# A memory-bound decode kernel: two loads for w4's apart rows, two for wo, and another order of the first loads on two issuing engines

## The chip, the cores and the metric

The kernel runs on one core of one Trainium2 chip. Times are device microseconds (us) of one execution. A timed execution is about 1.8 us longer than the span of the profile, which goes from the first to the last instruction.

## The reference

One decode step for four sequences, in bfloat16, with two branches on one normalised input:

```python
x  = A_x                                   # 4 x 1 x 576
xn = layernorm(x)
out = x + A(xn) + B(xn)

# A: attention over the last 2048 of 8192 cached positions; 32 query heads, 16 kv heads, 128 wide
q = xn @ wq                                # wq 576 x 4096
p = softmax(q @ k_window / sqrt(128))      # k, v: 4 x 16 x 2048 x 128
A = (p @ v_window) @ wo                    # wo 4096 x 576

# B: with one position, the shifted mixer part is zero, so x1 = xn
B = xn + gelu(layernorm(xn) @ w3) @ w4     # w3 576 x 4608, w4 4608 x 576
```

The K and V windows are 67 MB of the 87.17 MB that a run reads. Each weight is used for four rows only.

## The kernel before

Everything is streamed once from memory. The sync engine issues nearly all loads; six buffers of 2 MB hold K and V heads. The parts that the change and the argument touch:

```python
kvp = ctx.enter_context(tc.tile_pool(name="kv", bufs=NKV))        # NKV = 6
wop = ctx.enter_context(tc.tile_pool(name="wo", bufs=2))
# ... cut: the other pools
first = wop.tile([P, WOR * D], BF16, tag="wo", name="first")      # small things of the start share a wo buffer

# the first loads
x_bf = part(D, B)                                                 # a slice of "first"
nc.scalar.dma_start(out=x_bf[:], in_=x2)                          # 4.5 KB
nc.sync.dma_start(out=wq_sb[:, KJ * NQ:], in_=...)                # wq's last 64 rows, 128 pieces of 4096 bytes
nc.sync.dma_start(out=wq_sb[:, 0:KJ * NQ], in_=wq_main)           # 128 rows of 32,768 bytes

def load_wo(p):                                                   # a quarter of wo, one buffer
    t = wop.tile([P, WOR, D], BF16, tag="wo", name="wo_sb")
    nc.sync.dma_start(out=t[:].rearrange("p i n -> p (i n)"), in_=wo_src[p])

# 128 rows of w4 ("apart rows") are loaded by eight small DMAs: "A" 20 x 5 rows, "C" 12 rows, six of 2 or 4 rows
X_AFTER = {13: ["A", (0, 0, 4)], 14: [(1, 0, 4), (2, 0, 2), "C"], 15: [(2, 2, 4), (3, 0, 2), (3, 2, 4)]}

# the order of loads: K0 K1 K2 V0 K3 V1 K4 V2 ..., a wo quarter before V0, V4, V8, V12, w3 after V2, w4 last
def flush_loads():
    while pos["n"] < len(order) and pos["free"] > 0:
        kind, h = order[pos["n"]]
        if kind == "V" and h % WOQ == 0:
            load_wo(h // WOQ)
        # ... cut: load_kv(kind, h), and the apart rows after V13, V14 and V15
    if pos["n"] == len(order):
        pos["n"] += 1
        load_w4()                                                 # six pieces, the last two are small

# ... cut: 16 heads of scores, softmax and PV; the MLP's first product at head 7
# the end
mlp_extra(XC, XS)          # apart rows A and C, before the last head's PV
# ... cut: the last PV and its sums
mlp_extra(XB, XC)          # the single apart rows
o_proj(hl)
for lo, hi in pieces:
    mlp_out(lo, hi)        # w4, piece by piece as it lands
# ... cut: two halves of acc to fin
nc.sync.dma_start(out=o2, in_=fin[:])
```

Of the kernel before, what the change touches and what calls it, by code (L numbers as in the profile page):

```python
# [22 lines left out]
def kernel(  # L23
# [15 lines left out]
    P = 128  # L39
# [38 lines left out]
    wp = ctx.enter_context(tc.tile_pool(name="w", bufs=1))  # L78
    wop = ctx.enter_context(tc.tile_pool(name="wo", bufs=2))
    ktp = ctx.enter_context(tc.tile_pool(name="kt", bufs=2))  # L80
# [16 lines left out]
    WOQ = WOH // rep  # L97
    wo_src = A_wo.rearrange("(s p i) n -> s p (i n)", p=P, i=WOR)

# [6 lines left out]

    first = wop.tile([P, WOR * D], BF16, tag="wo", name="first")
    cut = {"at": 0}

    def part(n, parts=P):  # L110
# [3 lines left out]
        return first[0:parts, lo:lo + n]  # L114

    x_bf = part(D, B)
    nc.scalar.dma_start(out=x_bf[:], in_=x2)
    wq_sb = wp.tile([P, KJ * NQ + NQ // 2], BF16, tag="w", name="wq_sb")
    wq_main = A_wq[0:KJ * P, :].rearrange("(p j) n -> p (j n)", j=KJ)
    nc.sync.dma_start(out=wq_sb[:, KJ * NQ:], in_=A_wq[KJ * P:D, :].rearrange("r (e f) -> (r e) f", e=2))  # L120
    nc.sync.dma_start(out=wq_sb[:, 0:KJ * NQ], in_=wq_main)

    def load_wo(p):
        t = wop.tile([P, WOR, D], BF16, tag="wo", name="wo_sb")
        nc.sync.dma_start(out=t[:].rearrange("p i n -> p (i n)"), in_=wo_src[p])
        wo_tiles[p] = t
# [9 lines left out]
    X0 = F - P  # L136
    XB, XC, XA = 0, 4, 5
    XS = 10
    NX = 20
    NS = NFM + XS  # L140

    def x_cols(ap):
        b, c, a = ap[:, 0:16], ap[:, 16:28], ap[:, 28:P]
        return [(0, b.rearrange("p (q i) -> p i q", q=4)), (16, c.rearrange("p (q g) -> p g q", q=4)),
                (28, a.rearrange("p (q g i) -> p i g q", q=4, g=5))]

# [12 lines left out]

    def x4_rows(part):  # L160
        t = w_tiles["x4"]
        if part == "A":
            src = B_w4[X0 + 28:F, :].rearrange("(q g i) n -> g q (i n)", q=4, g=5)
            nc.sync.dma_start(out=t[0:NX, XA * D:XS * D], in_=src)
        elif part == "C":
            src = B_w4[X0 + 16:X0 + 28, :].rearrange("(q g) n -> g q n", q=4)
            nc.sync.dma_start(out=t[0:12, XC * D:XA * D], in_=src)
        else:
            q, lo, hi = part
            src = B_w4[X0 + 4 * q + lo:X0 + 4 * q + hi, :].rearrange("(q i) n -> q (i n)", q=1)  # L170
            nc.sync.dma_start(out=t[q:q + 1, (XB + lo) * D:(XB + hi) * D], in_=src)

    X_AFTER = {13: ["A", (0, 0, 4)], 14: [(1, 0, 4), (2, 0, 2), "C"], 15: [(2, 2, 4), (3, 0, 2), (3, 2, 4)]}

# [295 lines left out]
    def o_proj(h):  # L470
        if h % WOQ < WOQ - 1:
            return
        acc_matmuls([(op[:, i, :], wo_tiles[h // WOQ][:, i, :]) for i in range(WOR)])

# [35 lines left out]
    def mlp_turn(r):  # L510
# [9 lines left out]
        if r < 2:  # L520
            dst = xs[:, r * NFH:r * NFH + 16, :].rearrange("p (g u) b -> p u g b", u=n)
        else:
            e1 = slice(QD, 2 * QD)
            for s in range(XS):
                off, k = (4 * s, 4) if s < XC else (16, 12) if s == XC else (28 + NX * (s - XA), NX)
                nc.tensor.transpose(out=gT_all[0:k, n * m + s, :], in_=g_x[e1, off:off + k],
                                    identity=ident_f[e1, e1])
            for lo, hi, k in ((XB, XC, 4), (XC, XA, 12), (XA, XS, NX)):
                nc.scalar.activation(out=xs[0:k, NFM + lo:NFM + hi, :],
                                     in_=gT_all[0:k, n * m + lo:n * m + hi, 0:B], func=ACT.Copy)  # L530
            nc.scalar.activation(out=xs[:, NFM - 1, :], in_=gT_ps[:, 0, 1, 0:B], func=ACT.Copy)
            nc.scalar.activation(out=xs[:, 16:18, :], in_=gT_ps[:, :, 0, 0:B], func=ACT.Copy)  # L532
            return
# [10 lines left out]

    def mlp_extra(lo, hi):
        t = w_tiles["x4"]
        acc_matmuls([(gT[0:k, NFM + s, :], t[0:k, s * D:(s + 1) * D])
                     for s in range(lo, hi) for k in (4 if s < XC else 12 if s == XC else NX,)])

# [6 lines left out]
    for h in range(Hkv):  # L556
        order.append(("V", h))
        if h + 3 < Hkv:
            order.append(("K", h + 3))
        if h == min(X_AFTER):  # L560
            order.append(("X", h))
    W3_AFTER = ("V", 2)
    pos = {"n": 0, "free": NKV}

    def flush_loads():
        while pos["n"] < len(order) and pos["free"] > 0:
            kind, h = order[pos["n"]]
            if kind == "V" and h % WOQ == 0:
                load_wo(h // WOQ)
            if kind == "X":  # L570
                load_x4()
            else:
                load_kv(kind, h)
            if kind == "X" or kind == "V" and h > min(X_AFTER):
                for part in X_AFTER.get(h, []):
                    x4_rows(part)
            pos["n"] += 1
# [82 lines left out]
    o_scale(hl - 1)  # L660
    mlp_extra(XC, XS)
    for s in range(NSL):
# [8 lines left out]
    o_pick(hl)  # L671
    mlp_extra(XB, XC)
    o_proj(hl)
# [41 lines left out]
```

## Time and profile before

| | before |
|---|---|
| median, lowest to highest of the first 3 runs | 211.31 us, 211.28 to 212.18 |
| span of the profiled run, mean granted TensorE clock | 209.6 us, 0.868 |
| bytes read, rate over the span | 87.17 MB, 416 GB/s |
| busy share: PE, DVE, ACT | 72%, 54%, 17% |
| w4's first piece issued, last load complete | 189.67 us, 206.60 us |

Two more rows are needed: the page's part on DMA queues (packets, MB, and the time of their packets as a share of 16 engines' span) tells which ring carried what.

```profile
q1 hardware_dynamic: 6684, 87.17, 97.7%
q10 hardware_dynamic: 8, 0.00, 0.0%
```

q1 is the ring of the sync engine, q10 that of ScalarE. Before the change q10 carries x and nothing else. The table of busy time by stretches reads: stretch, us, then busy us and instructions of PE, PEld, DVE, ACT, POOL, then the granted clock, the DMA share and GB/s.

```profile
0.00:2.00 2.00, 0.00 (x0) 0.00 (x0) 0.60 (x2) 0.68 (x1) 1.26 (x9) 1.00 0.17 22
2.00:4.00 2.00, 0.00 (x0) 0.00 (x0) 1.01 (x4) 1.99 (x4) 0.17 (x3) 1.00 1.29 504
4.00:14.00 10.00, 3.45 (x23) 1.32 (x27) 4.19 (x16) 5.03 (x4) 5.26 (x16) 1.00 0.95 405
```

In the third stretch every engine is already at work: x is there at 2.9 us, long before wq.

### The profile page before, as it was taken

The numbers are of one execution on the slowest core, as the hardware profiler recorded it, in microseconds if no ns is written. First come the engines' busy times: TensorE is split into PE (matmuls) and PEld (weight loads), VectorE is DVE, ScalarE is ACT, GpSimd is POOL, SyncE is SP. The second block draws the span as 40 slices with busy tenths as digits, with TensorE's granted clock in tenths as the row PEclk, the third lists the DMA queues.
The fourth block names the chain that finished last, engine by engine and source line by source line (L and its number), as shares of the span: only waits on it lengthen the run. The fifth ranks groups of instructions, "written<-read, shape, count | busy, mean of one in ns | idle before, by whom it ended". The sixth has DMA issues, their size and how long they took to land.

```text
span 209.6 us, 2356 instructions
## 1 busy us (share of the span) xinstructions
PE 150.2 (72%) x958; PEld 58.2 (28%) x972; DVE 113.4 (54%) x156; ACT 34.8 (17%) x72; POOL 9.0 (4%) x32
## 2 busy tenths in 40 slices
PE   0357297699590039958998987589697955999693
PEld 0122132233140003213444332234232312343361
DVE  4511877894910083935608889176848390764200
ACT  7612201012010011110222221102111111023100
POOL 4710000000000000000002100000000000000000
PEclk9999589999787555788999999789978796699979
DMA  7999999999999999999999999999999999999992
GB/s 301 400 419 425 425 424 430 438 432 424 434 450 406 427 435 420 443 428 435 428 428 435 419 428 434 435 425 438 428 428 438 415 439 435 416 441 428 432 403 98
DMA packets 6702, 87.31 MB, mean 417 GB/s; under 512 B 758, under 2 KB 1034, under 8 KB 1700
## 3 DMA queue, kind: packets, MB, share of 16 engines
q1 hardware_dynamic: 6684, 87.17, 97.7%
q8 instruction: 7, 0.11, 0.2%
q10 hardware_dynamic: 8, 0.00, 0.0%
q14 instruction: 3, 0.02, 0.0%
HBM read 87.17 MB, written 0.00 MB: 416 GB/s over the span
## 4 chain that ended last, share of the span: by engine, by line
DMA 66%; DVE 15%; PE 14%; ACT 1%; issue 1%; SPq 1%; DVEq 0%; ACTq 0%
DMA kn<-in_A_k_cache_dram 43%; DVE kt L253 12%; DMA vn<-in_A_v_cache_dram 10%; DMA w_sb<-in_B_w_dram 7%; DMA wq_sb<-in_A_wq_dram 6%; PE S L366 5%; PE g_ps L496 2%; PE q_ps L310 2%; PE O L423 1%; PE oT L436 1%; DVE PT L400 1%; PE acc L212 1%; DVE mx L372 1%; PE S L388 1%; ACT E L395 1%
## 5 line engine op out<-in xcount | busy, mean ns | idle before, releaser
L366 PE MATMUL S<-kt,qz 128*128 128x512 bf16 x242 | 76.4, 437 | 32.2 <-DVE kt L253 30.4
L253 DVE STREAM_TRANSPOSE kt<-kn 128x2048 int32<-128x2048 int32 x32 | 73.4, 2297 | 24.3 <-DMA kn<-in_A_k_cache_dram 22.9
L366 PEld LDWEIGHTS <-qz 128*128 128x128 bf16 x256 | 23.5, 106 | 64.3 <-issue 47.7
L423 PE MATMUL O<-vn,PT 128*32 128x512 bf16 x256 | 23.9, 414 | 9.3 <-DMA vn<-in_A_v_cache_dram 9.3
L430 ACT ACTIVATE O_sb<-O,rd 128x512 f32<-128x512 f32 x16 | 11.0, 686 | 64.7 <-DVE rd L413 48.3
L395 ACT ACTIVATE E<-S 128x512 bf16<-128x512 f32 x16 | 9.5, 597 | 72.6 <-PE S L388 72.6
L400 DVE STREAM_TRANSPOSE PT<-E 128x512 bf16<-128x512 bf16 x16 | 11.4, 710 | 14.4 <-ACT E L395 14.4
L446 DVE TENSOR_REDUCE on<-oT 128x8 bf16<-128x128 f32 x16 | 4.6, 289 | 22.1 <-PE oT L436 21.9
L423 PEld LDWEIGHTS <-PT 128*32 128x32 bf16 x256 | 5.5, 95 | 33.0 <-issue 22.1
L436 PE MATMUL oT<-ident_w,O_sb 128*128 128x128 f32 x64 | 12.7, 331 | 0.3 <-ACT O_sb L430 0.3
L372 DVE TENSOR_REDUCE mx<-S 128x1 f32<-128x512 f32 x16 | 10.5, 659 | 1.1 <-PE S L366 1.1
L436 PEld LDWEIGHTS oT<-ident_w,O_sb 128*128 128x128 f32 x64 | 8.3, 165 | 5.2 <-issue 4.3
L388 PE MATMUL S<-nm,j_row 8*128 8x512 bf16 x16 | 6.7, 421 | 1.8 <-DVE nm L384 1.7
L354 PE MATMUL S<-negbig,ohT 4*128 4x512 bf16 x16 | 6.2, 384 | 0.0
L212 PE MATMUL acc<-w_sb,gT 128*4 128x288 bf16 x70 | 5.5, 311 | 0.6 <-DMA w_sb<-in_B_w_dram 0.6
L310 PE MATMUL q_ps<-wq_sb,xnT 128*32 128x512 bf16 x40 | 4.3, 611 | 2.2 <-DMA wq_sb<-in_A_wq_dram 2.2
L212 PE MATMUL acc<-wo_sb,op 128*4 128x288 bf16 x64 | 5.5, 324 | 0.4 <-DVE op L468 0.4
L496 PE MATMUL g_ps<-w_sb,ln2T 128*32 128x512 bf16 (+2 forms) x55 | 5.5, 441 | 0.0
L212 PEld LDWEIGHTS <-gT 128*4 128x4 bf16 (+3 forms) x90 | 4.2, 89 | 3.1 <-issue 1.0
L538 POOL TENSOR_TENSOR g_u<-g_x 128x180 f32<-128x180 f32 x1 | 0.5, 486 | 101.9 <-ACT g_x L532 101.9
L681 DVE CAST fin<-acc 4x288 bf16<-4x288 f32 x1 | 0.4, 446 | 8.1 <-PE acc L212 8.1
L534 DVE COPY g_x<-gT_ps 128x64 f32<-128x64 f32 x2 | 0.4, 223 | 7.5 <-PE gT_ps L518 7.5
(94 smaller groups left out, 79.3 us busy)
## 6 DMA issues: line engine op xcount, KB each, us to landing
kn<-in_A_k_cache_dram SPq DMA_DIRECT2D x16, 2048.0 KB, 25.9
vn<-in_A_v_cache_dram SPq DMA_DIRECT2D x16, 2048.0 KB, 22.7
wo_sb<-in_A_wo_dram SPq DMA_DIRECT2D x4, 1152.0 KB, 37.8
w_sb<-in_B_w_dram SPq DMA_DIRECT2D x1, 4608.0 KB
wq_sb<-in_A_wq_dram SPq DMA_DIRECT2D x1, 4096.0 KB
w_sb<-in_B_w_dram SPq DMA_DIRECT2D x1, 2592.0 KB, 11.0
w_sb<-in_B_w_dram SPq DMA_DIRECT2D x2, 576.0 KB, 34.3
w_sb<-in_B_w_dram SPq DMA_DIRECT2D x1, 864.0 KB
```

Of the source, the lines that this page charges most:

```text
L212: nc.tensor.matmul(out=acc_of(i), lhsT=lhsT, rhs=rhs[:, i * CW:(i + 1) * CW], start=False, stop=False, skip_group_check=True)
L253: nc.vector.transpose(out=kt[:], in_=src)
L310: nc.tensor.matmul(out=q_ps[r][g * QD:(g + 1) * QD, :], lhsT=xnT[:, k, :], rhs=wq_sb[:, col:col + NW], start=(j == 0), stop=False, skip_gr ...
L366: nc.tensor.matmul(out=S_ps[h][:], lhsT=qz[:, z0:z0 + P], rhs=kt[:, ib, c0:c0 + SC, e:2 * QD:2].rearrange("p c k -> p (c k)"), start=False ...
L372: nc.vector.reduce_max(out=mx[:], in_=S_ps[h][:], axis=AX.X)
L388: nc.tensor.matmul(out=S_ps[h][:], lhsT=j_row[:], rhs=st.pop(("nm", h))[:, 0:1].to_broadcast([NJ, NW]), start=False, stop=False, skip_grou ...
L395: nc.scalar.activation(out=E[h][:].rearrange("p c k -> p (c k)"), in_=S_ps.pop(h)[:], func=ACT.Exp, scale=scale, accum_out=st["rs"][:, h % ...
L400: nc.vector.transpose(out=PT[h][:], in_=E.pop(h)[:])
L423: nc.tensor.matmul(out=O_ps[h][g * QD:(g + 1) * QD], lhsT=PT[h][:, c, :], rhs=vn[:, :, c, :], start=(s == 0), stop=False, skip_group_check ...
L430: nc.scalar.activation(out=O_sb[h][:], in_=O_ps.pop(h)[:], func=ACT.Copy, scale=st.pop(("rd", h)))
L436: nc.tensor.transpose(out=oT[:, s, :], in_=o[:, s, :], identity=ident_w[:, s * NJ:s * NJ + P])
L496: nc.tensor.matmul(out=out, lhsT=ln2T[:, k, :], rhs=rhs, start=(j == 0), stop=False, skip_group_check=True)
```

## The change

Its intent is fewer and larger DMAs: wo comes in two loads and not four, the apart rows of w4 in two and not eight. The sync queue's first load becomes wq's main rows; wq's last 64 rows (the "tail") go to ScalarE's queue, and x behind them. The core of the diff:

```diff
-    wop = ctx.enter_context(tc.tile_pool(name="wo", bufs=2))
+    wop = ctx.enter_context(tc.tile_pool(name="wo", bufs=1))
-    wo_src = A_wo.rearrange("(s p i) n -> s p (i n)", p=P, i=WOR)
+    wo_src = A_wo.rearrange("(t s p i) n -> t p s (i n)", s=2, p=P, i=WOR)
     ...
-    x_bf = part(D, B)
-    nc.scalar.dma_start(out=x_bf[:], in_=x2)
-    nc.sync.dma_start(out=wq_sb[:, KJ * NQ:], in_=A_wq[KJ * P:D, :].rearrange("r (e f) -> (r e) f", e=2))
+    nc.scalar.dma_start(out=wq_sb[:, KJ * NQ:], in_=A_wq[KJ * P:D, :].rearrange("r (e f) -> (r e) f", e=2))
     nc.sync.dma_start(out=wq_sb[:, 0:KJ * NQ], in_=wq_main)
+    x_bf = part(D, B)
+    nc.scalar.dma_start(out=x_bf[:], in_=x2)
     ...
-    def x4_rows(part):
-        ...                                          (eight DMAs, spread over V13, V14 and V15)
+        for lo, hi, src in ((0, 1, B_w4[X0:X0 + XE, :].rearrange("(q g) n -> g q n", q=4)),
+                            (1, XS, B_w4[X0 + XE:F, :].rearrange("(q g i) n -> g q (i n)", q=4, g=5))):
+            nc.sync.dma_start(out=w_tiles["x4"][0:NX if lo else XE, lo * D:hi * D], in_=src)
     ...
+    WO_AT = [("V", 2), ("V", 12)]
-            if kind == "V" and h % WOQ == 0:
-                load_wo(h // WOQ)
+            if (kind, h) in WO_AT:
+                load_wo(WO_AT.index((kind, h)))
     ...
-    mlp_extra(XC, XS)
+    mlp_extra()                                      (all apart rows before the last PV)
     ...
-    mlp_extra(XB, XC)
```

The bytes stay the same.

More of the change, by code (lines that the diff above doesn't have):

```diff
@@ L105, in load_kv @@
         kv_tiles[kind, h] = t
-    first = wop.tile([P, WOR * D], BF16, tag="wo", name="first")
+    first = wop.tile([P, 2, WOR, D], BF16, tag="wo", name="first")[:].rearrange("p s i n -> p (s i n)")
     cut = {"at": 0}
@@ L114, in part @@
         return first[0:parts, lo:lo + n]
+    wq_sb = wp.tile([P, KJ * NQ + NQ // 2], BF16, tag="w", name="wq_sb")
+    wq_main = A_wq[0:KJ * P, :].rearrange("(p j) n -> p (j n)", j=KJ)
+    nc.scalar.dma_start(out=wq_sb[:, KJ * NQ:], in_=A_wq[KJ * P:D, :].rearrange("r (e f) -> (r e) f", e=2))
+    nc.sync.dma_start(out=wq_sb[:, 0:KJ * NQ], in_=wq_main)
     x_bf = part(D, B)
     nc.scalar.dma_start(out=x_bf[:], in_=x2)
-    wq_sb = wp.tile([P, KJ * NQ + NQ // 2], BF16, tag="w", name="wq_sb")
-    wq_main = A_wq[0:KJ * P, :].rearrange("(p j) n -> p (j n)", j=KJ)
-    nc.sync.dma_start(out=wq_sb[:, KJ * NQ:], in_=A_wq[KJ * P:D, :].rearrange("r (e f) -> (r e) f", e=2))
-    nc.sync.dma_start(out=wq_sb[:, 0:KJ * NQ], in_=wq_main)
     def load_wo(p):
-        t = wop.tile([P, WOR, D], BF16, tag="wo", name="wo_sb")
-        nc.sync.dma_start(out=t[:].rearrange("p i n -> p (i n)"), in_=wo_src[p])
+        t = wop.tile([P, 2, WOR, D], BF16, tag="wo", name="wo_sb")
+        nc.sync.dma_start(out=t[:].rearrange("p s i n -> p s (i n)"), in_=wo_src[p])
         wo_tiles[p] = t
@@ L136 @@
     X0 = F - P
-    XB, XC, XA = 0, 4, 5
-    XS = 10
+    XE, XS = 28, 6
     NX = 20
@@ L142, in x_cols @@
     def x_cols(ap):
-        b, c, a = ap[:, 0:16], ap[:, 16:28], ap[:, 28:P]
-        return [(0, b.rearrange("p (q i) -> p i q", q=4)), (16, c.rearrange("p (q g) -> p g q", q=4)),
-                (28, a.rearrange("p (q g i) -> p i g q", q=4, g=5))]
+        return [(0, ap[:, 0:XE].rearrange("p (q g) -> p g q", q=4)),
+                (XE, ap[:, XE:P].rearrange("p (q g i) -> p i g q", q=4, g=5))]
     def load_w4():
@@ L158, in load_x4 @@
         w_tiles["x4"] = t[:].rearrange("p c d -> p (c d)")
-    def x4_rows(part):
-        t = w_tiles["x4"]
-        if part == "A":
-            src = B_w4[X0 + 28:F, :].rearrange("(q g i) n -> g q (i n)", q=4, g=5)
-            nc.sync.dma_start(out=t[0:NX, XA * D:XS * D], in_=src)
-        elif part == "C":
-            src = B_w4[X0 + 16:X0 + 28, :].rearrange("(q g) n -> g q n", q=4)
-            nc.sync.dma_start(out=t[0:12, XC * D:XA * D], in_=src)
-        else:
-            q, lo, hi = part
-            src = B_w4[X0 + 4 * q + lo:X0 + 4 * q + hi, :].rearrange("(q i) n -> q (i n)", q=1)
-            nc.sync.dma_start(out=t[q:q + 1, (XB + lo) * D:(XB + hi) * D], in_=src)
-    X_AFTER = {13: ["A", (0, 0, 4)], 14: [(1, 0, 4), (2, 0, 2), "C"], 15: [(2, 2, 4), (3, 0, 2), (3, 2, 4)]}
+        for lo, hi, src in ((0, 1, B_w4[X0:X0 + XE, :].rearrange("(q g) n -> g q n", q=4)),
+                            (1, XS, B_w4[X0 + XE:F, :].rearrange("(q g i) n -> g q (i n)", q=4, g=5))):
+            nc.sync.dma_start(out=w_tiles["x4"][0:NX if lo else XE, lo * D:hi * D], in_=src)
     ident_bf = const.tile([P, P], BF16)
@@ L472, in o_proj @@
             return
-        acc_matmuls([(op[:, i, :], wo_tiles[h // WOQ][:, i, :]) for i in range(WOR)])
+        acc_matmuls([(op[:, i, :], wo_tiles[h // WOQ // 2][:, h // WOQ % 2, i, :]) for i in range(WOR)])
     G_CHUNKS = [(e, 4 * g, 4) for e in range(2) for g in range(NQD)] + [(e, 16, 2) for e in range(2)]
@@ L524, in mlp_turn @@
             for s in range(XS):
-                off, k = (4 * s, 4) if s < XC else (16, 12) if s == XC else (28 + NX * (s - XA), NX)
+                off, k = (XE + NX * (s - 1), NX) if s else (0, XE)
                 nc.tensor.transpose(out=gT_all[0:k, n * m + s, :], in_=g_x[e1, off:off + k],
                                     identity=ident_f[e1, e1])
-            for lo, hi, k in ((XB, XC, 4), (XC, XA, 12), (XA, XS, NX)):
+            for lo, hi, k in ((0, 1, XE), (1, XS, NX)):
                 nc.scalar.activation(out=xs[0:k, NFM + lo:NFM + hi, :],
@@ L543, in mlp_act, with mlp_extra @@
         nc.gpsimd.tensor_tensor(out=gT[:], in0=u[:], in1=xs[:], op=ALU.mult)
-    def mlp_extra(lo, hi):
+    def mlp_extra():
         t = w_tiles["x4"]
         acc_matmuls([(gT[0:k, NFM + s, :], t[0:k, s * D:(s + 1) * D])
-                     for s in range(lo, hi) for k in (4 if s < XC else 12 if s == XC else NX,)])
+                     for s in range(XS) for k in (NX if s else XE,)])
     def mlp_out(lo, hi):
@@ L559 @@
             order.append(("K", h + 3))
-        if h == min(X_AFTER):
+        if h == 13:
             order.append(("X", h))
     W3_AFTER = ("V", 2)
+    WO_AT = [("V", 2), ("V", 12)]
     pos = {"n": 0, "free": NKV}
@@ L573, in flush_loads @@
                 load_kv(kind, h)
-            if kind == "X" or kind == "V" and h > min(X_AFTER):
-                for part in X_AFTER.get(h, []):
-                    x4_rows(part)
             pos["n"] += 1
@@ L660 @@
     o_scale(hl - 1)
-    mlp_extra(XC, XS)
+    mlp_extra()
     for s in range(NSL):
```

## The prediction

> **What bounds the kernel now.** I read the page first: its three DMA rows, then the shares of the chain that ended last, then the stretches table for the last twenty microseconds, then the sync queue's timeline.
>
> ```profile
> DMA  7999999999999999999999999999999999999992
> GB/s 301 400 419 425 425 424 430 438 432 424 434 450 406 427 435 420 443 428 435 428 428 435 419 428 434 435 425 438 428 428 438 415 439 435 416 441 428 432 403 98
> q8 instruction: 7, 0.11, 0.2%
> HBM read 87.17 MB, written 0.00 MB: 416 GB/s over the span
> DMA 66%; DVE 15%; PE 14%; ACT 1%; issue 1%; SPq 1%; DVEq 0%; ACTq 0%
> ```
>
> From the second slice to the last but one the 16 DMA engines are never below nine tenths busy, near 428 GB/s. No kernel that reads the same 87.17 MB can end much before this stream does: 87.17 MB / 430 GB/s is 202.7 us, the first packet starts at 1.7 us, and the last load is complete at about 206.6 us. The rest of the 209.6 us is a fixed tail.
>
> ```profile
> 184.00:190.00 6.00, 6.00 (x51) 2.46 (x54) 3.27 (x5) 0.69 (x2) 0.00 (x0) 1.00 1.02 436
> 195.00:200.00 5.00, 3.97 (x50) 2.15 (x40) 1.43 (x4) 0.69 (x1) 0.00 (x0) 0.87 0.94 399
> 200.00:204.00 4.00, 4.00 (x52) 2.55 (x48) 0.00 (x0) 0.00 (x0) 0.00 (x0) 0.73 1.00 415
> 204.00:206.00 2.00, 1.39 (x22) 0.77 (x18) 0.00 (x0) 0.00 (x0) 0.00 (x0) 1.00 0.82 316
> ```
>
> The last two columns are DMA share and GB/s. The stream runs on while w4 is being issued (184 to 204 us, share 0.94 to 1.02), and falls to 0.82 only in the last two microseconds, when some engines have finished and others have not. The completion events of the last w4 piece show that spread: 16 events, one per engine, over 1.79 us; four engines are early by 1.5 us or more, eleven lie within 0.45 us of the last.
>
> ```profile
> 167.94 21.71 DMA vn<-in_A_v_cache_dram
> 189.67 0.36 SPq L153
> 191.35 14.53 DMA w_sb<-in_B_w_dram
> 205.92 1.05 PE acc L212 x12
> 206.97 0.43 DVE fin L681
> ```
>
> These are the last pieces of the chain (start, us, what). It seems to say that w4's issue waited for a V load (189.65 us) and that an earlier issue would end the kernel earlier. It would not: V14 is complete at 189.65, V15 only at 194.5 by its events, and w4's first piece follows on the same busy queue.
>
> ```profile
> 27.00 0.53 SPq L103 DMA_DIRECT2D kn<-in_A_k_cache_dram  x1
> 33.89 0.53 SPq L103 DMA_DIRECT2D vn<-in_A_v_cache_dram  x1
> 13.92 1.47 PE L310 MATMUL q_ps<-wq_sb,xnT 128*32 128x512 bf16 x12 [2.16 <-DMA wq_sb<-in_A_wq_dram]
> 2.92 0.45 DVE L217 BATCH_NORM_STATS2 st<-first 4x6 f32<-4x288 bf16 x1 [1.44 <-DMA first<-in_A_x_dram]
> ```
>
> K4, the first load that waits for a buffer, is issued at 27.00 us, when V1, last of those queued before it, lands at 47.4: the queue holds 20 us of work. Later backlogs are 17 to 26 us, falling to 9.8 before V15 and 4.9 before w4 (189.67 against 194.5). The last two lines are for the start: x starts the layernorms at 2.92, and the q matmuls wait 2.16 us for wq, so x has slack.
>
> **What the Trainium skill says.** All from the page "DMA: Bandwidth & Descriptors". Its section "Issuing engines are not separate DMA queues" says that loads from ScalarE and from the sync queue run on the same 16 engines and that a second issuer saves only issue time; the trace has 0.40 us for that issue. "Queues, rings and completion order" says that each engine takes turns between rings with work, a whole packet at a time; the trace of before has two long transfers on two rings nowhere, so it does not settle what a turn is. "Why a DMA increments its semaphore by 16 and not by 1" says that a copy uses the largest k up to 16 that divides the slowest dimension on both sides, on the lowest-numbered engines; the trace agrees: the 20-row part of x4 completes in five events, the 12-row part in three, the single rows in one.
>
> **The change part by part.**
> 1. *Start.* Removed: one 0.40 us issue ahead of wq's main rows. But the tail it issued must still arrive, and both rings now start at once near 1.7 us. wq in all is 4.72 MB either way, 11 us at 430 GB/s, so wq is complete near 13.9 as before. Gain 0 to 0.1 us.
> 2. *x behind wq's tail.* On engines 0 to 3, x comes after 8 tail rows of 4096 bytes. If one ring alone drained, x would land at 3 to 5 us. If the engine alternates one 32,768-byte row (1.21 us, median of the packet records) with one 4096-byte row (0.16 us), x lands after 8 x 1.37 = 11 us, near 12.7. The weights of the first q matmul are loaded at 11.69, so PE needs x + 8.8 us (11.7 - 2.9); q would start at 21.5 and not 13.9, 7.6 us late. K4's issue moves from 27.0 to 34.6. In the new order V1 lands one wo quarter (1.18 MB, 2.7 us) earlier, near 44: the backlog is still 9 us. The compute makes it up while it waits for data before 96 us. Cost at the end: 0.
> 3. *Ring switches.* Where an instruction fetch of 16,384 bytes slips between two rows of the stream, its record takes 0.88 to 1.00 us against 0.61 for a data row of that size, and the next data row mostly 0.5 longer. For an 8,192-byte fetch on another ring the fetch takes 0.31, but the next row 0.24 to 0.53 longer. If each of 8 alternations cost 0.45, every engine would lose 3.6 us. With both rings full I expect most of it to be hidden: 0.3 us.
> 4. *wo by two.* Same 512 rows of 9216 bytes. The first pair must wait for the last reader of the start tile (about 20 us before, 28 at worst after), but stands in the queue behind K4. The second waits for the projection after head 7, as the fourth load does now (145.24 us). Data between moves by 2.7 us one way or the other, under the backlogs. Cost 0.
> 5. *Apart rows by two DMAs.* Engine 0 carries 40 rows of 1152 bytes now (20 + 4 + 16), engines 1 and 2 have 24, 3 and 4 have 20. After: 0 to 4 have 24, 5 and 6 have 4. Engine 0 loses 16 x 0.047 = 0.75 us, which would matter only if it ended last alone: its events put it, after its last single, 1.7 us behind the earliest, level with the engines that took an instruction fetch (seven fetches, each worth about 1.4 us). Those stay. Engines 5 and 6 gain 4 x 0.047 = 0.19 us each, which shows only if one of them is among the late. Estimate 0 to +0.2, say +0.1.
> 6. *Seven fewer DMAs at the end*, so w4 no longer waits for completion counters of tiny loads and is issued some 5 to 15 us earlier. The queue never ran dry, so 0.
> 7. *Matmuls.* Eight of 4x288 leave the end (0.65 us at 197.9), but PE waits 0.61 us for w4's fourth piece at 205.92 all the same: 0. The MLP turn saves four transposes and two ScalarE copies at 98 to 118 us, also under the backlog: 0.
>
> Sum: -0.05 + 0 + 0.3 + 0 + 0.1 + 0 + 0 = +0.35. 211.31 + 0.35 = **211.7 us**.
>
> **The rivals.**
> - *Alternating rings waste the engines.* For it: the lengthened rows beside fetches. Against it: those come from a ring that was idle before, and land elsewhere. It would make 213 to 215.
> - *The late start empties the queue.* If q came 15 us late rather than 7.6, K4 would be issued at 42 and the stream would have almost no backlog left. That needs x later than the whole of wq, with further delay in the layernorms. It would add 1 to 5 us: 212.5 to 216. I give it little.
> - *The earlier issue of w4 and a lighter engine 0 pay.* For it: the chain's pieces at 189.67 and the 0.82 share at the end. If engine 0 alone ended last, removing its surplus would give at most 0.1 us before the next engine, so 211.0 to 211.2.
>
> **Range and chances.** The stream pins the time from below: I see no more than 0.5 us to win, so 210.8 is the low end. Upwards the ring rival has a long tail, so 214.0. Faster by over 2% would need 207.1 us, below what the same bytes allow with this tail: 0.01. Slower by over 2% needs 215.5, the full ring loss or an empty queue: 0.09. Within 2%: 0.90.
>
> **What would show it.** Right: HBM read stays 87.17 MB, the DMA row stays at nine from the second slice on, w4 is issued well before 189 us, and the last PE group still begins near 206. The wait of the first batch-norm row tells when x landed (about 5 or 12 us), and K4's issue should be later by just the delay of q. Wrong: a slice with DMA below nine between 20 and 200 us (an empty queue), wq complete well after 14 us (ring losses), or a last load that completes more than 1 us before 206.6 with the same bytes.

## More of the kernel before

The experiments came in three batches (e1 to e4, e5 to e8, e9 to e11), each on another chip. The kernels of one batch ran on the same chip and share the runs of the kernel before, so a ratio is always taken inside a batch.

## The result, and the profile after

| | before | after |
|---|---|---|
| median of 6 runs each (lowest to highest) | 211.28 us (211.14 to 212.18) | 211.65 us (211.54 to 211.82) |
| ratio, 95% interval | | 1.0012 (0.9995 to 1.0029) |
| span of the profiled run, clock | 209.6 us, 0.868 | 209.9 us, 0.935 |

A ratio is the mean time of one kernel's runs over that of the other's of the same rounds, so it is not quite the ratio of the medians, which are 0.37 us apart. The interval includes 1, so these runs alone do not show that the change costs anything.

The page of the kernel after, in the order in which the prediction read the one before: DMA rows, queue rows, bytes, chain.

```profile
DMA  6999999999999999999999999999999999999992
GB/s 237 450 401 450 428 422 450 415 431 419 429 464 443 398 434 418 447 425 428 434 428 431 434 415 445 425 428 437 428 431 416 428 451 422 429 433 437 421 400 81
q10 hardware_dynamic: 152, 0.53, 0.8%
HBM read 87.17 MB, written 0.00 MB: 415 GB/s over the span
DMA 51%; DVE 16%; PE 14%; ACT 1%; issue 1%; ACTq 0%
```

The stream is still without a slice below nine between the second and the last but one, and the bytes are the same. The first slice (5.2 us) is weaker, 237 GB/s against 301, and the second is stronger. Most of that is made good, as the table of stretches for the start shows:

```profile
0.00:2.00 2.00, 0.00 (x0) 0.00 (x0) 0.60 (x2) 0.22 (x1) 1.26 (x9) 1.00 0.24 39
2.00:4.00 2.00, 0.00 (x0) 0.00 (x0) 0.00 (x0) 1.99 (x4) 0.17 (x3) 1.00 0.92 299
4.00:14.00 10.00, 0.00 (x0) 0.00 (x0) 0.00 (x0) 3.04 (x1) 0.00 (x0) 1.00 1.01 434
```

Multiply GB/s by the width of each stretch: up to 4 us the kernel before had moved (22 + 504) x 2 us = 1.05 MB, the kernel after (39 + 299) x 2 us = 0.68 MB; in the next 10 us it is 4.05 against 4.34 MB. At 14 us the kernel after is 0.09 MB behind, about 0.2 us of stream. PE and DVE are idle through the whole third stretch, because x is not there. The timeline of the kernel after (start, us, engine, operation) says when things come:

```profile
14.26 0.45 DVE L204 BATCH_NORM_STATS2 st<-first 4x6 f32<-4x288 bf16 x1 [12.77 <-DMA first<-in_A_x_dram]
23.03 3.84 PE L297 MATMUL q_ps<-wq_sb,xnT 128*32 128x512 bf16 x40
35.71 0.54 SPq L103 DMA_DIRECT2D kn<-in_A_k_cache_dram  x1
170.95 15.35 SPq L151 DMA_DIRECT2D w_sb<-in_B_w_dram  x6
```

x starts the layernorms at 14.26 us and not at 2.92, q starts 9.1 us later, K4 is issued 8.7 us later, and w4's first piece is issued 18.7 us earlier than 189.67. Neither the delay nor the head start is to be found at the end. The chain of waits now ends so:

```profile
154.86 30.14 DMA vn<-in_A_v_cache_dram
185.02 21.04 DMA w_sb<-in_B_w_dram
206.10 0.78 PE acc L199 x10
...
207.21 0.43 DVE fin L665
```

The chain no longer passes through the sync queue's issue of w4, but its last pieces begin at 206.10 and 207.21, where they began at 205.92 and 206.97. PE waits for w4's fourth piece just as before, 0.62 us here and 0.61 there:

```profile
206.10 1.07 PE L199 MATMUL acc<-w_sb,gT 128*4 128x288 bf16 x12 [0.62 <-DMA w_sb<-in_B_w_dram]
```

The last load is complete at 206.84 us, against 206.60. So most of the profiled 0.3 us is there when the last engine ends its part of the stream. As a mean over the 16 engines the last piece lands at 206.02 us, against 206.01, so the stream as a whole is not later. The question for the experiments was whether these tenths come from the start or from the end.

### The profile page after: what moved, and what is told of

The parts are those of the page before. It is cut to its first block, busy times and chain, and to the rows that moved or that the text cites. A ratio compares the mean times of both kernels' runs of the same rounds, so it can differ in the third digit from the quotient of the medians.

```text
span 209.9 us, 2335 instructions
## 1 busy us (share of the span) xinstructions
PE 140.8 (67%) x960; PEld 55.1 (26%) x960; DVE 113.6 (54%) x156; ACT 34.7 (17%) x70; POOL 8.9 (4%) x32
## 4 chain that ended last, share of the span: by engine, by line
DMA 51%; DVE 16%; PE 14%; ACT 1%; issue 1%; ACTq 0%
DMA vn<-in_A_v_cache_dram 25%; DMA kn<-in_A_k_cache_dram 15%; DVE kt L240 13%; DMA w_sb<-in_B_w_dram 10%; PE S L353 6%; PE g_ps L483 2%; PE O L410 2%; DVE mx L359 1%; ACT E L382 1%; PE S L375 1%; DVE PT L387 1%; PE acc L199 1%; PE oT L423 1%; DVE dm L361 1%; PE gT_ps L505 1%
## 5 line engine op out<-in xcount | busy, mean ns | idle before, releaser
L353 PE MATMUL S<-kt,qz 128*128 128x512 bf16 x256 | 72.7, 410 | 31.2 <-DVE kt L240 31.2
L353 PEld LDWEIGHTS <-qz 128*128 128x128 bf16 x256 | 22.6, 101 | 62.4 <-issue 43.4
L410 PE MATMUL O<-vn,PT 128*32 128x512 bf16 x256 | 22.9, 400 | 8.4 <-DMA vn<-in_A_v_cache_dram 8.4
L417 ACT ACTIVATE O_sb<-O,rd 128x512 f32<-128x512 f32 x16 | 11.0, 686 | 62.4 <-DVE rd L400 47.4
L410 PEld LDWEIGHTS <-PT 128*32 128x32 bf16 x256 | 5.6, 94 | 29.7 <-issue 21.4
L224 PE MATMUL tp<-ident_bf,first 4*128 4x4 bf16 x8 | 0.6, 172 | 16.7 <-DVE first L211 16.7
L423 PE MATMUL oT<-ident_w,O_sb 128*128 128x128 f32 x64 | 11.3, 303 | 0.3 <-ACT O_sb L417 0.3
L423 PEld LDWEIGHTS oT<-ident_w,O_sb 128*128 128x128 f32 x64 | 7.4, 152 | 4.8 <-issue 4.1
L204 DVE BATCH_NORM_STATS2 st<-first 4x6 f32<-4x288 bf16 x2 | 0.9, 443 | 12.8 <-DMA first<-in_A_x_dram 12.8
L199 PE MATMUL acc<-w_sb,gT 128*4 128x288 bf16 x70 | 4.9, 285 | 2.0 <-DMA w_sb<-in_B_w_dram 2.0
L199 PE MATMUL acc<-wo_sb,op 128*4 128x288 bf16 x64 | 4.6, 286 | 1.0 <-DVE op L455 1.0
L199 PEld LDWEIGHTS <-gT 128*4 128x4 bf16 (+2 forms) x82 | 3.6, 83 | 4.0 <-issue 2.8
```

The lines of the kernel that those rows point to most:

```text
L199: nc.tensor.matmul(out=acc_of(i), lhsT=lhsT, rhs=rhs[:, i * CW:(i + 1) * CW], start=False, stop=False, skip_group_check=True)
L353: nc.tensor.matmul(out=S_ps[h][:], lhsT=qz[:, z0:z0 + P], rhs=kt[:, ib, c0:c0 + SC, e:2 * QD:2].rearrange("p c k -> p (c k)"), start=False ...
L410: nc.tensor.matmul(out=O_ps[h][g * QD:(g + 1) * QD], lhsT=PT[h][:, c, :], rhs=vn[:, :, c, :], start=(s == 0), stop=False, skip_group_check ...
L417: nc.scalar.activation(out=O_sb[h][:], in_=O_ps.pop(h)[:], func=ACT.Copy, scale=st.pop(("rd", h)))
L423: nc.tensor.transpose(out=oT[:, s, :], in_=o[:, s, :], identity=ident_w[:, s * NJ:s * NJ + P])
```

## The experiments

Letters in the expectations are working names of theories. **A**: the new start loses some time because two rings share each engine. **B**, its rival: the end loses it, through the apart rows. **C** is an effect of wo's order or of nothing in particular. **D**, **E** and **F** came later: D is a refill of the sync engine's instructions, E says that the time follows the DMA queue alone, F is the order of the waits that close the program. "Before + ..." means the kernel before with one edit.

| run | kernel | median us (n) | kernel before, same batch | ratio (95%) |
|---|---|---|---|---|
| e1_start_only | before + new start | 211.68 (5) | 211.48 | 1.0013 (1.0001 to 1.0025) |
| e2_apart_only | before + apart rows by two | 212.19 (6) | 211.48 | 1.0038 (1.0025 to 1.0052) |
| e3_wo_only | before + wo by two | 211.38 (5) | 211.48 | 0.9996 (0.9984 to 1.0008) |
| e4_all_but_start | after, with the old start | 211.43 (6) | 211.48 | 1.0009 (0.9991 to 1.0028) |
| e5_apart_plus1 | e2 with one DMA more | 211.86 (6) | 211.30 | 1.0020 (1.0007 to 1.0034) |
| e6_after_plus3 | after with three DMAs more | 212.60 (6) | 211.30 | 1.0059 (1.0044 to 1.0075) |
| e7_x_then_tail | before, tail on ScalarE's queue behind x | 211.56 (6) | 211.30 | 1.0015 (0.9999 to 1.0030) |
| e8_x_after_k1 | before, x behind K1 | 215.27 (4) | 211.30 | 1.0183 (1.0167 to 1.0199) |
| e9_x_after_k0 | before, x behind K0 | 211.71 (6) | 211.24 | 1.0027 (1.0002 to 1.0051) |
| e10_tail_in_four | e7 with the tail in four loads | 212.17 (6) | 211.24 | 1.0039 (1.0026 to 1.0053) |
| e11_wo_plus2 | e3 with two DMAs more | 211.40 (6) | 211.24 | 1.0003 (0.9987 to 1.0018) |

All gave the right result. The kernel before was run 11 times in each batch.

### e1: the new start alone

```diff
-    x_bf = part(D, B)
-    nc.scalar.dma_start(out=x_bf[:], in_=x2)
-    nc.sync.dma_start(out=wq_sb[:, KJ * NQ:], in_=...)
+    nc.scalar.dma_start(out=wq_sb[:, KJ * NQ:], in_=...)
     nc.sync.dma_start(out=wq_sb[:, 0:KJ * NQ], in_=wq_main)
+    x_bf = part(D, B)
+    nc.scalar.dma_start(out=x_bf[:], in_=x2)
```

> The kernel before with the new start alone (wq's last 64 rows and then x from ScalarE's queue, wq's main rows first on the sync queue). Theory A, the start: while the two rings share the engines, four engines fall some 0.6 us behind the others, three of these later take an instruction fetch as well, and the last w4 piece then spreads over 2.1 us instead of 1.8. It expects +0.3 to +0.4 us (about 211.6), x landing near 14.2, K4 issued near 35, the last load near 206.9. Theory B, the apart rows: engines 5 and 6 now carry four of them each and one of the two is a late engine. It expects 211.3 here. Theory C, an effect of wo's order or of nothing in particular (noise of builds): 211.3 as well.

It cost 0.20 us by the medians, 0.27 us by the ratio (0.0013 x 211.5). x started DVE at 15.46 us and K4 was issued at 37.33 us, later still than in the kernel after.

The packet records of the traces (one row of a transfer each, with its ring, start and duration) show when the stream loses it. A row of the tail usually takes 159 ns, a row of wq's main part 1213 ns. The sum of what the rows of wq take beyond that, divided by the 16 engines, is 0.44 us in the kernel before, 0.40 in e2, 0.38 in e3 and 0.42 in e4, which all have the old start. It is 0.75 us in the kernel after, 0.75 in e1 and 0.71 in e7, which load wq over two rings: **0.33 us more**. It is not spread over the turns: of the 128 main rows 11 in the kernel after and 15 in e1 took 1.5 to 2.2 us, at the very beginning, and the others 1.21 to 1.28. K0, the load behind wq, completes at 18.52 to 18.61 us (mean of the 16 engines) in the kernel before, e2, e3 and e4, and at 18.80 to 18.84 in the kernel after, e1 and e7 (in e10, told below, at 18.53, when most of its tail is still to come).

The same records speak against turns between the rings as the cause. In e1 the 15 long rows start between 1.78 and 2.14 us, and the first row on ScalarE's ring starts only at 3.64 us; in e7 the tail's first row starts at 6.05 us. Adding up the bytes of the rows (each spread evenly over its duration, at 430 GB/s) gives how far a kernel's stream is behind that of the kernel before: at 5 us 0.30 us in the kernel after, 0.34 in e1 and 0.30 in e7, and hardly less at 10 us (0.26, 0.30, 0.27). The kernels with the old start stay within 0.08 us of it at both times. So in e7 the loss is complete before a row of the tail has moved. The kernel before has a second ring at its start as well: x's four rows, from 1.66 us on. What else the new starts share is that rows of 32,768 bytes, and not of 4096, are the sync ring's first. No run puts the main rows first on a single ring, so it is not shown which of the two costs the 0.3 us.

At the end of the stream the difference is only just visible: the last load is complete at 206.75 to 206.91 us in the four kernels with the new start (after, e1, e6, e7) and at 206.55 to 206.85 in the seven with the old one (all but e8). The spread of the last w4 piece over the engines, by which A and B were to be told apart, decided nothing: 1.98 us in e1, 1.97 in e2, 2.03 in e3, 1.94 in e4.

### e2: the apart rows alone

```diff
-    (eight DMAs of apart rows, spread over V13 to V15; ten small products, the single rows' ones after the last PV)
+    (two DMAs after V13; six products, all before the last PV, as in the change)
```

> The kernel before with the two DMAs for the apart rows of w4 alone. Theory A (the start): 211.3, at most +0.1, spread of the last w4 piece 1.8 to 1.9 us, although w4 is issued 10 us or more earlier. Theory B (apart rows on engines 5 and 6): +0.2 to +0.4 us, spread 2.0 us or more. A gain from the earlier issue of w4, which the chain of before suggests, would be 211.0 or less.

It cost 0.71 us, twice as much as the whole change of which it is a part. A had expected at most 0.1 us, B at most 0.4. The timeline of e2 at the end:

```profile
207.21 0.45 DVE L664 CAST fin<-acc 4x288 bf16<-4x288 f32 x1 [8.09 <-PE acc L199]
208.14 0.32 SPq L667 DMA_DIRECT2D out_dram<-fin  x1
```

The kernel before has, at the same place:

```profile
206.96 0.45 DVE L681 CAST fin<-acc 4x288 bf16<-4x288 f32 x1 [8.11 <-PE acc L212]
207.47 0.29 SPq L684 DMA_DIRECT2D out_dram<-fin  x1
```

The result is ready when the cast ends: 207.66 us in e2, 207.41 in the kernel before. Between that and the output's DMA lie 0.48 us in e2 and 0.06 in the kernel before. And from the landing of the output to the end of the span it takes 1.02 us against 0.83. So e2 loses three things: 0.25 us when the last load comes, 0.42 us ahead of the output, and 0.19 us behind it. Their sum is 0.86 us; the spans differ by 0.96 (210.55 and 209.59), and the other 0.1 us is the output's own way, 1.38 us from issue to landing against 1.28. The first of the three does not come with the apart rows: e4 and e5 have the same two DMAs and complete their last load at 206.58 and 206.55 us. None of the others is in the prediction, and the whole change shows neither.

The sequencer's records gave a theory for the second. In eleven of the thirteen traces the sync engine makes one late pause of 0.45 to 0.46 us, always ahead of the same instruction by number, the 80th of its program (waits counted); in e5 and e9 a longer gap (3.8 and 4.3 us) stands there and would hide it. A fetch of 8192 bytes of instructions starts 0.6 to 4.3 us after each of these pauses. The output's DMA is number 86 in the kernel before, 85 in e1, 84 in e3, 81 in e5, **80 in e2 and e6**, 78 in e4 and 77 in the kernel after. That is theory D: the change takes instructions out of the sync engine's program, and how many decides where the pause falls. That the pause is a refill is only a guess from the fetch that follows it; the experiments below test its place, not its nature.

Theory F is for the third. The loads of the sync engine use eight completion counters in turn. After the output's DMA the sync engine goes through five more waiting instructions, always in the same order, 0.065 to 0.07 us apart, and these cover the counters. The number of DMAs decides which counter the output gets: its wait is the last of the five in the kernel before, the second in e2. What stands behind it (three waits, 0.19 us) comes after the landing; what stands ahead of it is done while the output is under way.

### e3: wo by two alone

```diff
-    wop = ... bufs=2;  one load of 128 x 9216 bytes before V0, V4, V8, V12
+    wop = ... bufs=1;  one load of 2 x 128 x 9216 bytes before V2 and before V12
```

> The kernel before with wo in two loads of twice the size alone (before V2 and before V12). Theories A and B: 211.3, within 0.1 us, as the bytes are the same and the queue does not run dry. Theory C (order of the wo loads): +0.3.

The ratio is 0.9996: nothing. Its last load completes, as a mean over the engines, 0.2 us earlier than that of the kernel before (205.82 against 206.01), as does e4's; I have no cause for that, and with one trace each it is within the scatter of the traces.

### e4: all but the start

```diff
 (kernel after)
+    x_bf = part(D, B)
+    nc.scalar.dma_start(out=x_bf[:], in_=x2)
-    nc.scalar.dma_start(out=wq_sb[:, KJ * NQ:], in_=...)
+    nc.sync.dma_start(out=wq_sb[:, KJ * NQ:], in_=...)
     nc.sync.dma_start(out=wq_sb[:, 0:KJ * NQ], in_=wq_main)
-    x_bf = part(D, B)
-    nc.scalar.dma_start(out=x_bf[:], in_=x2)
```

> The changed kernel with the start of the kernel before (x alone on ScalarE's queue, wq's last rows first on the sync queue). Theory A: 211.3, and q starts at 13.9 again. Theory B: about 211.6, as with the whole change.

The median is 0.05 us below that of the kernel before, the ratio is 1.0009 with an interval across 1. With both parts of the end in it, no loss can be told from the scatter (two of its six runs took 211.89 and 212.53 us). The 0.71 us of e2 is gone although the apart rows are the same: the output's DMA is number 78, so the pause falls among the closing waits, and the output's counter is in the last of the five waits (0.85 us from landing to end).

### e5: e2 with one DMA more

```diff
 (e2: before + apart rows by two)
-        nc.sync.dma_start(out=dst, in_=src)
+        if kind == "K" and h == 0:
+            nc.sync.dma_start(out=dst[:, 0:half], in_=src[:, :, 0:half])
+            nc.sync.dma_start(out=dst[:, half:], in_=src[:, :, half:])
+        else:
+            nc.sync.dma_start(out=dst, in_=src)
```

> The kernel with the apart rows by two DMAs alone (0.7 us slower than before in the last runs), with K0's load cut into two halves, so that the sync queue has one instruction more. Theory D: that kernel lost 0.44 us because a refill of the sync queue's instructions fell exactly in front of the output's DMA (issued at 208.14, though the result was ready at 207.66); in all six traces the pause of 0.42 to 0.48 us stands before the same instruction by count. With one more, the pause falls into the long wait for w4 and is hidden: 0.4 to 0.6 us faster than without it, 211.5 to 211.7, output issued 0.05 us after the result. Rival (the two DMAs' rows unbalance the engines): stays near 212.2.

K0 in two halves brings no byte more, but one sync instruction. The timeline at the end:

```profile
206.92 0.45 DVE L670 CAST fin<-acc 4x288 bf16<-4x288 f32 x1 [8.13 <-PE acc L205]
207.46 0.32 SPq L673 DMA_DIRECT2D out_dram<-fin  x1
```

The gap ahead of the output fell from 0.48 to 0.10 us (207.46 less 207.36, where the cast ends before rounding). The output's counter is now in the first of the five waits, and it takes 1.08 us from landing to end. The time is 0.56 us above the batch's kernel before, where e2's was 0.71, and above the 211.5 to 211.7 us that D expected. D is borne out for the gap, much less so on the clock. What e5 still loses is 0.25 us of F (1.08 against 0.83) and 0.2 to 0.3 us, by the ratio or the medians, that its profile does not show: there the cast begins level with that of the kernel before. The profiled run was the fastest of the six, 211.63 us.

### e6: the kernel after with three DMAs more

```diff
 (kernel after)
+        if kind == "K" and h < 3:                       (K0, K1 and K2 in two halves each)
+            nc.sync.dma_start(out=dst[:, 0:half], in_=src[:, :, 0:half])
+            nc.sync.dma_start(out=dst[:, half:], in_=src[:, :, half:])
```

> The changed kernel with the loads of K0, K1 and K2 cut into halves, so that the sync queue has three instructions more, which puts the same instruction count in front of the output's DMA. Theory D: 0.4 to 0.6 us slower than the changed kernel, 212.1 to 212.3, output issued some 0.45 us after the result is ready. Rival: the count of sync instructions means nothing, 211.6 to 211.8.

This is D's other direction: three instructions put the output's DMA from number 77 to 80.

```profile
207.22 0.45 DVE L671 CAST fin<-acc 4x288 bf16<-4x288 f32 x1 [8.14 <-PE acc L205]
208.15 0.32 SPq L674 DMA_DIRECT2D out_dram<-fin  x1
```

The kernel after has, for the same two steps, the cast done at 207.65 and this issue:

```profile
207.73 0.31 SPq L668 DMA_DIRECT2D out_dram<-fin  x1
```

The cast is level with the kernel after, and the output leaves 0.42 us later. From landing to end it takes 1.09 us instead of 0.86 (the output's counter is in the first wait, not in the last). That is 0.65 us in the profile, and the output's own way takes another 0.1 us (1.40 us from issue to landing against 1.29); the spans differ by 0.77 (210.65 and 209.88). The timed difference to the kernel after is 0.95 us by the medians of two batches, more than D's 0.4 to 0.6; the remaining 0.2 us I can't place, but the profiled run was the fastest of its six. D's pause can thus be put in front of the output and taken from it at will.

### e7: x first, then the tail, on ScalarE's queue

```diff
     nc.scalar.dma_start(out=x_bf[:], in_=x2)
-    nc.sync.dma_start(out=wq_sb[:, KJ * NQ:], in_=...)
+    nc.scalar.dma_start(out=wq_sb[:, KJ * NQ:], in_=...)
     nc.sync.dma_start(out=wq_sb[:, 0:KJ * NQ], in_=wq_main)
```

> The kernel before with x first on ScalarE's queue and wq's last rows behind it there, wq's main rows first on the sync queue. Two rings still share the engines at the start, but x is early. Theory A (as it stands now: the first rows of two cold rings, 0.3 us per engine): 211.6 to 211.8, x at 3, q at 13.9 to 14.5, K0 complete 0.2 to 0.3 us later than before. Rival (the late x and the late start of the compute cost the time): 211.3 to 211.4.

This keeps wq on two rings and gives x its early place back:

```profile
2.67 0.45 DVE L217 BATCH_NORM_STATS2 st<-first 4x6 f32<-4x288 bf16 x1 [1.18 <-DMA first<-in_A_x_dram]
13.90 3.71 PE L310 MATMUL q_ps<-wq_sb,xnT 128*32 128x512 bf16 x40 [2.39 <-DMA wq_sb<-in_A_wq_dram]
```

q starts at 13.90 us, where the kernel before has 13.92. The time is 0.26 us above the kernel before all the same (ratio 1.0015, its interval just touching 1). So what the new start costs comes with the loads of wq, and x's delay of 11 us costs nothing that these runs resolve. Whether it is the second ring or the main rows in front is not separated (see e1).

### e8: x behind K1

```diff
-    nc.scalar.dma_start(out=x_bf[:], in_=x2)
     nc.sync.dma_start(out=wq_sb[:, KJ * NQ:], in_=...)
     nc.sync.dma_start(out=wq_sb[:, 0:KJ * NQ], in_=wq_main)
+    LATE = 2
+    for h in range(LATE):
+        load_kv("K", h)
+    x_bf = part(D, B)
+    nc.sync.dma_start(out=x_bf[:], in_=x2)
     ...
-    pos = {"n": 0, "free": NKV}
+    pos = {"n": LATE, "free": NKV - LATE}
```

> The kernel before with x on the sync queue behind K1, so that it lands near 23.9 instead of 2.9 (14.3 in the changed kernel). By the prediction's backlog argument K4 is issued 21.4 us after x, at 45.3, and V1 lands at 47.4: the queue does not run dry and the time stays at 211.3 to 211.5 although q is 19 us late. Rival (a later compute start comes out at the end, in whole or in part): 214 or more.

This drives the prediction's second rival on purpose: x on one ring, behind two K loads. The backlog argument said that the queue would just hold. It did not.

```profile
23.53 0.45 DVE L220 BATCH_NORM_STATS2 st<-first 4x6 f32<-4x288 bf16 x1 [22.05 <-DMA first<-in_A_x_dram]
45.38 0.54 SPq L103 DMA_DIRECT2D kn<-in_A_k_cache_dram  x1
52.25 0.54 SPq L103 DMA_DIRECT2D vn<-in_A_v_cache_dram  x1
```

```profile
44.00:46.00 2.00, 1.98 (x5) 0.72 (x5) 1.35 (x1) 0.00 (x0) 0.00 (x0) 0.50 0.54 229
46.00:48.00 2.00, 2.00 (x9) 0.81 (x8) 1.30 (x1) 0.00 (x0) 0.00 (x0) 0.89 0.77 262
52.00:54.00 2.00, 1.69 (x8) 0.61 (x8) 0.82 (x3) 0.69 (x2) 0.00 (x0) 1.00 0.36 107
```

The DMA share falls to 0.54 around 45 us and to 0.36 at 52 us. There are two gaps. K4, issued at 45.38, came as the engines were about to be done with V1 (its events lie between 45.45 and 45.92 us). V2 was issued 6.9 us after K4, and K4 keeps the engines only 4.9 us. By the bytes moved, the stream falls 1.8 us further behind the kernel before from 44 to 48 us and 1.9 us from 52 to 56, and hardly more after that. The kernel lost 3.9 us by the ratio, 4.0 by the medians, so the two gaps are nearly all of it.

### e9: x behind K0

```diff
 (as e8, with)
+    LATE = 1
```

> The kernel before with x on the sync queue behind K0 (one place earlier than in the last run, where the queue ran dry at 45 and again at 52 us and 3.9 us were lost). x lands near 19, K4 should be issued near 40.5 and V2 near 47.5, V1 lands at 45.6 to 47.4 and K4 at 50.5 to 52: no gap either time. Theory E (the time follows the queue alone): 211.3 to 211.5 although q is 14 us later than before. Rival (each us of late compute costs part of a us at the end, as 21 us cost 4): 213 to 214.

```profile
18.65 0.45 DVE L220 BATCH_NORM_STATS2 st<-first 4x6 f32<-4x288 bf16 x1 [17.17 <-DMA first<-in_A_x_dram]
40.52 0.54 SPq L103 DMA_DIRECT2D kn<-in_A_k_cache_dram  x1
```

Here K4 is issued at 40.52 us and V2 at 47.50, and the DMA share of every stretch of 2 us from 44 to 56 us is 0.92 to 1.09: no gap in the profiled run, which took 211.46 us. Four of the six runs took 211.2 to 211.8 us, two 212.6 and 212.9; what the two lost is left open. x may come 16 us late at a cost of 0.47 us by the medians and 0.57 by the ratio (interval 0.04 to 1.1 us), more than the 0 to 0.2 us that E expected; 5 us more cost 3.9.

### e10: the tail in four loads

```diff
 (e7: x first, then the tail, on ScalarE's queue)
-    nc.scalar.dma_start(out=wq_sb[:, KJ * NQ:], in_=wq_tail)
+    for lo in range(0, NQ // 2, NQ // 8):
+        nc.scalar.dma_start(out=wq_sb[:, KJ * NQ + lo:KJ * NQ + lo + NQ // 8], in_=wq_tail[:, lo:lo + NQ // 8])
```

> As the run with x first and wq's last rows behind it on ScalarE's queue (211.56), but with those rows in four loads of 1024-byte rows: 32 turns per engine between the rings instead of 8. Theory A (only the first rows of the cold rings are longer): the same within 0.2 us, 211.5 to 211.8, K0 complete at 18.8 on the mean; some 0.1 us for the shorter rows. Rival (each turn between rings costs something): 24 more turns at 0.04 us, 212.5 or more.

The tail's 8 rows of 4096 bytes per engine become 32 of 1024, so there are four times as many turns between the rings. The time went up to 212.17 us, between what A (211.5 to 211.8) and its rival (212.5 or more) expected. But of the 0.6 us by which it is above e7, only part can be a matter of turns: 0.25 us is F (the output's counter is in the first wait, 1.08 us from landing to end), and a row of 1024 bytes takes 46 ns, more than a quarter of 159. The last load comes 0.50 us later than in e7 as a mean over the engines, which is at most 0.02 us for each of the 24 turns more. The prediction's worst case of 0.45 us a turn is far off. The four loads were complete at 14.6 to 29.7 us (means of the 16 engines): one row a turn.

By the bytes moved, even that is not spread over the turns. At 10 us e10 is 0.22 us behind the kernel before, much as e7 is; at 14 us, after 8 of the 32 turns, it is 0.60 us behind; at 30 us, after the other 24, still 0.60. I have no cause for the loss between 10 and 14 us. One more thing differs from e7: the last q matmuls wait for the tail's last quarter until 29.96 us and K4 is issued at 40.00, as late as in e9. The DMA share of every stretch from 40 to 54 us is 0.97 to 1.05, so the queue did not run dry.

### e11: e3 with two DMAs more

```diff
 (e3: before + wo by two)
+        if kind == "K" and h < 2:                       (K0 and K1 in two halves each)
```

> wo in two loads alone (211.38, ratio 0.9996) with K0 and K1 in halves, so that the output's DMA gets the last of the eight completion counters and the closing waits need no further step after it. Theory F (each closing wait after the output's own costs 0.065 us; two of them go): 0.1 us faster than with wo in two alone, 211.2 to 211.3, and 0.83 instead of 0.96 us from the output's landing to the end. It is also the best candidate against both kernels; I expect it no more than 0.1 us under the kernel before.

By F the output's counter should move from the third of the five waits to the last. From landing to end it took 0.84 us, against 0.96 in e3: as expected. The time did not follow (1.0003 against 0.9996); a gain of 0.1 us is below what five rounds resolve. No kernel beats both the kernel before and the kernel after by more than the scatter.

## Why the prediction was right

The time (211.7 against 211.65) and the sum (+0.35 against +0.37 by the medians) were right, and so was the main reason: the stream of the same bytes fixes the time as long as the queue holds. That the sum came so near is partly luck, as +0.37 us is not clear of the scatter and two of the terms in it rest on other causes than those given (steps 3 and 5). Step by step:

1. **Start, gain of 0 to 0.1 us:** none. The first row of wq starts at 1.77 us, before at 1.76, and wq is complete at 14.38 us and not near 13.9 (before 13.88).
2. **x behind the tail, cost 0:** right, with times that were 1 to 2 us too early. The alternation of one long and one short row was the right choice of the two; x started DVE at 14.26 and not near 12.7, q at 23.03 and not at 21.5, K4 at 35.71 and not at 34.6. The tail's eight rows were not late, their last ended at 10.88 to 11.67 us; but the four bytes that complete the tail came one turn later (12.09 to 12.88) and x's rows one turn after that (13.30 to 13.56), so the step counted two turns too few. V1 landed at 44.5 (near 44; the step's own 47.4 - 2.7 is 44.7), so the backlog was 8.8 us (9). e7 against e1 shows that the delay costs nothing that can be measured.
3. **Ring switches, +0.3 us:** right in size, 0.33 us per engine by the packet records and 0.26 us at K0, and e1 and e7 have it on the clock with 0.2 to 0.3 us, each with an interval that begins at about 1. The reason was wrong, so the size was luck. It isn't a price of each alternation, most of it hidden: the loss is there at 5 us, in e7 before the tail's first row, and in e10 24 turns between 14 and 30 us add nothing. It is in the first rows of wq; why they are longer is open.
4. **wo by two, 0:** right (e3).
5. **Apart rows, +0.1 us for the engines' loads:** this is the weak step. In the whole change no loss of that size can be told from scatter (e4). Alone the part costs 0.71 us (e2), of which 0.61 us in its profile has two reasons that the step did not look at: the sync engine's pause, 0.42 us, and the order of the closing waits, 0.19 us. The whole change is spared both because its output's DMA happens to be number 77 of the sync program and not 80, and its counter in the last wait. The step looked at bytes per engine and left out instructions, so its small number was partly luck.
6. **w4 issued earlier, 0:** right, though the apart rows lose six DMAs (eight become two) and not seven. It was issued 18.7 us earlier, beyond the 5 to 15 expected, and the last load ended no sooner.
7. **Matmuls, 0:** right. PE waits 0.62 us for the fourth piece where it waited 0.61.

A few readings in the prediction are slightly off, with no effect on the sum: of the four early engines three are early by 1.5 us or more and one by 1.46; the backlogs before V15 and w4 are 9.7 and 4.8 us; and the events of the apart rows' DMAs show how many engines work on each, not which.

Of the rivals, the first (ring waste of 2 us and more) falls with e10. The second is real but was set too tight in one place and too loose in another: it wanted K4's issue at 42 us or q 15 us late. e9, with K4 at 40.5 us, had no gap and lost about 0.5 us; e8, at 45.4 us, lost 3.9 us, because it is not only the first waiting load that counts: V2 came 6.9 us behind K4, longer than K4 lasts. The third rival's gain was nowhere to be seen, since w4 waits behind a full queue however early it is issued.

Shown by experiments: that the new start costs some 0.2 to 0.3 us (e1 and e7 agree, though their intervals begin at 1.0001 and 0.9999) and that this is not per turn (e7, e10), the pause and its place (e2, e5, e6), the limit of x's delay (e8, e9). Shown in traces only: the order of the closing waits. Open: whether the first rows take longer for the second ring or for the main rows in front; what the pause is; where e10 loses 0.4 us between 10 and 14 us; the 0.2 us that e6 and the 0.2 to 0.3 us that e5 lose on the clock beyond their profiles; e9's two long runs.

## What to carry to other kernels

In this kernel, which keeps its DMA engines full from end to end, fewer DMAs, an earlier issue and a later first input were all worth nothing that could be measured as long as the queue held work. In such a kernel, work out the backlog for the first waiting load and for the next one, since the second can empty the queue when the first does not. Once the stream is fixed, look at the tenths of a microsecond behind it: here the number of instructions on the issuing engine decided whether its pause of 0.45 us stood in front of the output, and the number of DMAs which counter the output waited on. Judge one part of a change on its own with care, since here a part cost twice what the whole did, most of it by shifting the counts of instructions and DMAs.

## What the Trainium skill lacked or had wrong

- "DMA: Bandwidth & Descriptors", section "Queues, rings and completion order", gives about 9 to 17 descriptors as what an engine typically drains from one ring before it switches. Here the turn was one row: the tail's 8 rows of 4096 bytes per engine, alternating with rows of 32,768 bytes, were complete at 12.4 to 13.2 us, and 32 rows of 1024 bytes lasted until 29.7 us (e10). The write of 4 bytes that completes the tail took a turn of its own (12.09 to 12.88 us).
- The same page, section "Issuing engines are not separate DMA queues", counts only the saved issue time for a second issuer. Here the split of wq over two issuers also decided when small things came: the 4.5 KB of x, behind 512 KB on the second ring, started DVE at 14.26 us instead of 2.92. The first rows of wq cost 0.33 us per engine more with the new start; that the second ring is the cause is not shown.
- "Runtime: NRT & Kernel Launch", section "Instruction fetch mechanics", has refills in blocks of 16 KiB and calls the crossing mostly hidden. Seven fetches here are 16,384 bytes, but three are 8192, and one of these follows the sync engine's pause in every trace where the pause is seen. If the pause belongs to that fetch, which is not shown, the crossing was not hidden: it stood open in front of the output in two kernels (e2, e6), for 0.42 us each.
- No page that I found has the waits that close a program: 0.065 to 0.07 us each, in a fixed order, so that the end came 0.83 to 1.10 us after the output's landing, depending on which of the five waits covers the output's counter.
- No page has what an instruction fetch does to the stream: in the kernel before a fetch of 16,384 bytes takes 0.88 to 1.00 us, and after most of them a data row of that size starts that takes 1.09 to 1.16 us and not 0.61.
